# Retention and top-2 experts on one Trainium2 core: gathered rows transposed ahead of the next chunk's rows, weight sums ahead of routing steps, third-sequence routing behind the first expert products

## Chip, core and metric

The kernel runs on one core of one Trainium2 chip. The metric is the device time of one execution in microseconds (us), lower being better. Three runs of the kernel before gave 706.69, 709.57 and 719.4 us, a median of 709.57.

## What is computed

A retention layer (a linear attention with a decay for each head) over 4 sequences of 768 tokens feeds a mixture of 8 experts, of which every token takes the best 2. Cut to its core:

```python
for t in range(S):                       # retention, 4 sequences, 8 heads of 64
    state = gamma * state + k[:, :, t, :, None] * v[:, :, t, None, :]
    y[:, :, t] = scale * einsum('bhd,bhde->bhe', q[:, :, t], state)
x = y as rows of 512                      # 3072 tokens
noisy = x @ w_gate + log1p(exp(x @ w_noise)) * noise
top2, weights = best two of 8 and their softmax
for e in range(8):                        # 512 -> 1024 -> 512
    out[mask] += weight * (relu(x[mask] @ w1[e]) @ w2[e])
```

## The kernel before

**Two phases.** The first runs over 24 chunks of 128 tokens, 6 for each of the four sequences (b = 0 to 3). The second runs over the experts: gather the rows of an expert's tokens, transpose them, two products, scale, add into the output by an indirect DMA. Expert 0 is split into pieces by the order in which its tokens become known: slots 0 to 383 come from the first two sequences, slots to 575 from the third, the rest from the fourth. So its work can start before the routing of the last tokens is finished.

**A chunk.** In the loop of lines 682 to 706, pass j issues: the score products of chunk j+1 (`qk`, L311), the scaled values and queries on POOL (`v_scale`, `q_scale`, L285, L291), the loads of chunk j+4 on SP (L226), the finishing of chunk j-1 (`x_hi` on ACT L350, `x_lo` on VectorE L354, `x_out` on SP: a transposing DMA L359 and a store to `xbuf` L360), the masked scores of chunk j+1 (`masked`, VectorE L318), whatever the table `between` holds for j, the products of chunk j (`y_mm`, L325 to L336, then copies of the state and a sum of squares on ACT, L342 and L345), the router logits of chunk j-3 (L366, L369), and whatever the table `todo` holds for j. Every engine runs its own instructions in exactly that order; nothing is reordered later. A row that waits holds up all rows behind it on its engine.

**Routing of a sequence** is a chain of small steps: `route_a` (logits out of PSUM, L379 to L388), `route_b` and `route_b2` (the best two, L396 to L418), `places` (running counts on TensorE, L425, L428), `route_c`, `route_h` (gates, L435 to L454), `route_d` (slots, L461 to L483), `route_e` and `products` (one-hot tables, L494, L496, L503), `table` (12 matmuls, L513), `route_f` (adds the table into `acc`, L520), `slots` (token numbers and weights, L526 to L536). After `slots` an indirect DMA on POOL gathers rows of `xbuf` (`gather`, L626), and a transposing DMA on SP writes them as columns into `xe` (`x_t`, L633).

**Weights of expert 0** are brought in during the chunk phase. `w_load` (SP, L176) fetches a quarter, `w_sum` (ACT, L180) sums its squares, `w_scale` adds the four sums over the partitions by a matmul (L184) into a corner of the PSUM tile `pR` and makes a power-of-two scale of them on VectorE, `w_hi` (ACT, L197) and `w_lo` (VectorE, L202) split the weights into two float16 parts. For the second matrix the low parts are made by `w_lo_pool`: a scaling on ACT (L209) and a subtraction on POOL (L210). The tile `pR` also holds the tables (L513) and the running counts.

**Between the phases** (lines 787 to 845) a list `units` holds the products of expert 0's early pieces: eight `mm1` of 384 columns (L729 to L731, then ACT L732 and VectorE L733), three `mm2` (L759 to L761, then ACT L745), eight `mm1` of 192 columns, one more `mm2`. `early(n)` issues the next n of them. The routing steps of the third and fourth sequence are written between the calls. Before, nine units are issued ahead of `table` of the third sequence, and two more ahead of `table` of the fourth. After the fourth table come the gathers of the last piece, the expert order (`ranks`), its loads into registers on SP (L848) and the loads of expert 1's weights (L850, L851, issued by L176). PSUM tiles for `mm1` rotate through three buffers (`pA`, shared with the scores), so the fourth `mm1` waits until VectorE has finished with the first.

Of the kernel before, what the change touches and what calls it, by code (L numbers as in the profile page):

```python
# [19 lines left out]
B, H, S, D = 4, 8, 768, 64  # L20
C = 128
NC = S // C
NCH = B * NC
# [11 lines left out]
B0 = B // 2  # L35
# [59 lines left out]
def moe_kernel(ctx, tc, qT, kT, kt, vt, noise, wgn, w1, w2, ctab, qtab, xbuf, out):  # L95
    nc = tc.nc
# [29 lines left out]
    onef = consts.tile([128, 128], F32, name="onef")  # L126
# [22 lines left out]
    SUM = pR[:, 480:488]  # L149
# [15 lines left out]
    ST, order = {}, []  # L165
# [13 lines left out]
        st, ss, sc = ST[which, e]  # L179
        nc.scalar.activation(junk, st[:, i * 1024:(i + 1) * 1024], AF.Square, accum_out=ss[:, i:i + 1])  # L180

    def w_scale(e, which):
        st, ss, sc = ST[which, e]
        nc.tensor.matmul(SUM[:, :4], onef, ss, start=True, stop=True, skip_group_check=True)  # L184
        s1 = work.tile([128, 1], F32, name="s1")
        nc.vector.tensor_reduce(s1, SUM[:, :4], axis=AX.X, op=OP.add)
        pow2(s1, TW1 if which == "1" else TW2, sc[:, 0:1], sc[:, 1:2])
# [17 lines left out]
    def w_lo_pool(e, which, i):  # L205
        st, ss, sc = ST[which, e]
        hi, lo = w_parts(which, i)
        s = st[:, i * 1024:(i + 1) * 1024]
        nc.scalar.activation(s, s, AF.Copy, scale=sc[:, 0:1])  # L209
        nc.gpsimd.tensor_tensor(lo, s, hi, op=OP.subtract)  # L210
# [151 lines left out]
    def logits(j):  # L362
        b, c = divmod(j, NC)
        v = int(b >= B0)
        for i in range(KT):
            nc.tensor.matmul(PL[:, c].rearrange("p s e -> p (s e)"), XT[j][:, i, :],  # L366
                             wg2[:, v, i].rearrange("p s e -> p (s e)"), start=(i == 0), stop=False,
                             skip_group_check=True)
            nc.tensor.matmul(PL[:, c, 0, :], XT[j][:, KT + i, :], wg2[:, v, i, 0, :], start=False, stop=(i == KT - 1),  # L369
                             skip_group_check=True)  # L370
# [85 lines left out]
    def route_d(b):  # L456
        oh, g, gr, cb, vv = R[b]
        s3 = [128, NC, NL]
        ov = work.tile(s3, F32, name="ov")
        sl = work.tile(s3, F32, name="sl")  # L460
        nc.vector.tensor_tensor(ov, POS[:, :NC, :], cb[:, 0:1, :].to_broadcast(s3), op=OP.is_ge)  # L461
        nc.vector.tensor_tensor(sl, POS[:, :NC, :], cb[:, 1:2, :].to_broadcast(s3), op=OP.add)
        ps = work.tile(s3, F32, name="ps")
        nc.vector.tensor_tensor(ps, POS[:, :NC, :], R["cum"][:, None, :].to_broadcast(s3), op=OP.add)
        nc.vector.scalar_tensor_tensor(ov, ov, BIG, sl, op0=OP.mult, op1=OP.add)
        cn = work.tile([128, NL], F32, name="cum")
        nc.vector.tensor_tensor(cn, POS[:, NC, :], R["cum"], op=OP.add)
        if b == B0 - 1:
            nc.vector.tensor_scalar(cn[:, E:E + 1], cn[:, 0:1], float(FIRST), None, op0=OP.max)
        if b == B - 2:  # L470
            nc.vector.tensor_scalar(cn[:, E + 1:NL], cn[:, E:E + 1], float(SECOND), None, op0=OP.max)
        R["cum"] = cn
        t = work.tile([128, 2, NC, NL], F32, name="t")
        nc.vector.tensor_tensor(t, oh, ov[:, None].to_broadcast([128, 2, NC, NL]), op=OP.mult)
        sf = work.tile([128, 2, NC], F32, name="sf")
        nc.vector.tensor_reduce(sf, t, axis=AX.X, op=OP.add)
        si = work.tile([128, 2, NC], I32, name="si")
        nc.vector.tensor_copy(si, sf)
        lb = work.tile([128, 2, 2, NC], I32, name="lb")
        nc.vector.tensor_scalar(lb[:, 0], si, 127, None, op0=OP.bitwise_and)  # L480
        nc.vector.tensor_scalar(lb[:, 1], si, 7, None, op0=OP.arith_shift_right)
        lf = work.tile([128, 2, 2, NC], BF, name="lf")
        nc.vector.tensor_copy(lf, lb)  # L483
        R[b] = (oh, g, ps, lf, vv)

    def route_e(b, k):

        if k == 0:
            R[b] += (work.tile([128, 2, NC, 128], BF, name="a", bufs=1),
                     work.tile([128, 2, NC, NV, NCOL], BF, name="bb", bufs=1),  # L490
                     work.tile([128, 2, NC, NCOL], BF, name="ob", bufs=1))
        oh, g, ps, lf, vv, a, bb, ob = R[b]
        s3 = [128, NC, NCOL]
        nc.vector.tensor_tensor(ob[:, k], blks[:, None, :].to_broadcast(s3), lf[:, 1, k, :, None].to_broadcast(s3),  # L494
                                op=OP.is_equal)
        nc.vector.tensor_tensor(a[:, k], lanes[:, None, :].to_broadcast([128, NC, 128]),  # L496
                                lf[:, 0, k, :, None].to_broadcast([128, NC, 128]), op=OP.is_equal)
        products(b, k, nc.vector, 0, 3)
# [68 lines left out]
    def route_g(b):  # L567

        oh, g, ps, lf, vv, a, bb, ob = R[b]
        sl = slice(b * NC, (b + 1) * NC)  # L570
        t = work.tile([128, 2, NC, NL], F32, name="t")
        nc.vector.tensor_tensor(t, oh, g[:, :, :, None].to_broadcast([128, 2, NC, NL]), op=OP.mult)
        nc.vector.tensor_tensor(gateb[:, sl], t[:, 0], t[:, 1], op=OP.add)
        t2 = work.tile([128, NC, NL], F32, name="t2")
        nc.vector.tensor_tensor(t2, oh[:, 0], oh[:, 1], op=OP.add)
        nc.vector.tensor_scalar(t2, t2, -BIG, BIG, op0=OP.mult, op1=OP.add)
        nc.vector.tensor_tensor(posb[:, sl], t2, ps, op=OP.add)
# [29 lines left out]
    todo = {}  # L607

    def at(j, f, *a):
        todo.setdefault(j, []).append((f, a))  # L610
# [25 lines left out]
    between = {}  # L636
    for b in range(B - 1):
        n = (b + 1) * NC
        steps = [(2, route_a, b), (3, route_b, b), (4, route_b2, b), (4, route_c, b), (4, route_h, b), (5, route_d, b),
                 (6, route_e, b, 0), (7, route_e2, b, 0), (7, route_e, b, 1), (8, route_e2, b, 1), (9, route_f, b),  # L640
                 (8, route_g, b)]
        if b == B - 2:
            steps = [(2, route_a, b), (3, route_b, b), (3, route_b2, b), (4, route_c, b), (4, route_h, b), (5, route_d, b)]
        else:
            between.setdefault(n + 9, []).append((table, b))
        between.setdefault(n + 5, []).append((places, b))
        if b == B0 - 1:

            steps = steps[:-2]
            between[n + 9] += [(route_f, b), (slots, 0, 3)]  # L650
            between[n + 9] += [(gather, 0, t, 0, 128, B0 * S) for t in range(2)]
            between.setdefault(n + 10, []).append((gather, 0, 2, 0, 128, B0 * S))
        for s in steps:
            at(n + s[0], *s[1:])
    at(0, gate_sum)
    at(1, gate_weights)
    for i in range(4):
        at((4, 7, 10, 12)[i], w_load, 0, "1", i)
        at((6, 9, 12, 14)[i], w_sum, 0, "1", i)
        at((15, 16, 17, 18)[i], w_hi, 0, "1", i)  # L660
        at((18, 19, 20, 22)[i], w_lo, 0, "1", i)
        at((14, 16, 17, 18)[i], w_load, 0, "2", i)
        at((16, 18, 19, 20)[i], w_sum, 0, "2", i)
        at(21 + i // 2, w_hi, 0, "2", i)
    at(2, nc.vector.tensor_copy, lanes, K("lanes"))
    at(2, nc.vector.tensor_copy, blks, K("blks"))
    between.setdefault(15, []).append((w_scale, 0, "1"))
    between.setdefault(21, []).append((w_scale, 0, "2"))
    at(22, w_lo_pool, 0, "2", 0)
    between[NCH - 1].append((w_lo_pool, 0, "2", 1))  # L670
    for t in range(2):
        at(NCH - 2, x_t, 0, t)
    between[NCH - 1].append((x_t, 0, 2))
    mid = SECOND // 128
    at(1, nc.sync.dma_start, xbuf[:128, :], zero.bitcast(F16))

# [31 lines left out]
    x_hi(NCH - 1)  # L708
    x_lo(NCH - 1)
    x_out(NCH - 1)  # L710
    route_g(B0 - 1)
    for i in range(7):
        zero_out(i)
    lctx.close()
# [20 lines left out]
    def out_scale(e, n0, n1):  # L735
        i2 = work.tile([128, 1], F32, name="i2")
        nc.vector.tensor_tensor(i2, ST["1", e][2][:, 1:2], ST["2", e][2][:, 1:2], op=OP.mult)
        if e not in GS:
            GS[e] = work.tile([128, NBLK], F32, name="gse")
        nc.vector.tensor_scalar(GS[e][:, n0:n1], wacc[:, NBLK * e + n0:NBLK * e + n1], i2, None, op0=OP.mult)  # L740
# [46 lines left out]
    b = B - 1  # L787
# [5 lines left out]
    def early(n):  # L793
        for _ in range(n):
            if units:
                units.pop(0)()

    w_lo_pool(0, "2", 2)
    w_lo_pool(0, "2", 3)
    early(1)  # L800
    logits(NCH - 3)
    route_e(b - 1, 0)
    products(b - 1, 0, nc.vector, 3, NV)
    early(1)
    logits(NCH - 2)
    early(2)
    logits(NCH - 1)
    route_a(b)
    early(1)
# [4 lines left out]
    products(b - 1, 1, nc.vector, 3, NV)  # L814
    early(2)
    places(b)
    out_scale(0, 0, 3)
    early(1)
    table(b - 1)
    route_c(b)  # L820
# [33 lines left out]
    for e in range(E):  # L854
        half = (CAPS[e] + 31) // 32 * 16
        cols = [(SECOND, CAPS[0])] if e == 0 else [(0, half), (half, CAPS[e])]
        n, more = 0, e + 1 < E
# [33 lines left out]
        todo = list(range(mid, NBLK)) if e == 0 else list(blocks(e))  # L891
# [30 lines left out]
    with tc.For_i(0, n_more) as i:  # L922
# [49 lines left out]
        for f in range(FT):  # L972
            ph = psum.tile([128, 128], F32, name="ph", tag="pA", bufs=3)
            for k in range(KT):
                nc.tensor.matmul(ph, w1t[:, k, f * 128:(f + 1) * 128], xt[:, k, :],
                                 start=(k == 0), stop=(k == KT - 1))
# [44 lines left out]
```

## Time and profile before

| | before |
|---|---|
| runs, median (lowest to highest) | 709.57 us (706.69 to 719.4) |
| the profiled execution | 707.5 us |
| its span, first to last instruction | 705.2 us |
| TensorE (PE) busy | 664.9 us, 94% |
| VectorE (DVE) busy | 300.8 us, 43% |
| ScalarE (ACT) busy | 298.3 us, 42% |
| GpSimd (POOL) busy | 220.9 us, 31% |
| chain that ended last | PE 80%, DVE 9%, DMA 4%, ACT 2%, SP's queue 2% |

The span is 2.3 us shorter than the execution's own time. The first 145 us are the chunk phase, the rest the experts, with expert 0's early pieces in between. PEclk is the granted clock of TensorE, 1.00 being full. In rows of the timeline the two numbers in front are the start and the length in us, and the bracket at the end is the idle time of that engine ahead of the row with what ended it. A row with x16 stands for 16 instructions.

### The profile page before, as it was taken

How to read it: one execution, taken by the hardware profiler on the slowest of the kernel's cores; microseconds unless marked ns; L12 is line 12 of the kernel's file. 1: busy time of each engine (PE TensorE's matmuls, PEld its weight loads, DVE VectorE, ACT ScalarE, POOL GpSimd, SP SyncE). 2: the span in 40 equal slices, each digit the busy share in tenths (PEclk: the TensorE clock that was granted, in tenths of full speed). 3: DMA queues.
4: the chain of work that ended last, by engine and by line, in shares of the span. 5: the costliest groups of instructions: out<-in, count | busy, mean ns of one | idle time of the engine just before them, and what ended most of it. 6: DMA issues, size and time to landing. Idle time of an engine off the chain costs nothing.

```text
span 705.2 us, 12301 instructions
## 1 busy us (share of the span) xinstructions
PE 664.9 (94%) x4949; PEld 411.2 (58%) x4949; DVE 300.8 (43%) x731; ACT 298.3 (42%) x540; POOL 220.9 (31%) x170
## 2 busy tenths in 40 slices
PE   8998798859999999999999999999999999999991
PEld 5998687735675554555455546554654565456540
DVE  4557969678743534352216221522252153215100
ACT  4553454452126743354344543544453554344110
POOL 4544635340352312420432044114302330330021
PEclk9999998779999999999999999999999999999997
DMA  9999999469289874676477266826672674472132
GB/s 329 318 319 323 358 345 298 122 152 355 46 222 257 149 239 74 111 178 165 79 132 217 95 120 115 275 35 115 107 270 47 127 203 135 75 132 32 16 46 31
DMA packets 116139, 119.25 MB, mean 169 GB/s; under 512 B 82609, under 2 KB 82865, under 8 KB 112497
## 3 DMA queue, kind: packets, MB, share of 16 engines
q1 hardware_dynamic: 104112, 91.25, 46.1%
q0 software_dynamic: 11392, 26.35, 20.2%
q8 instruction: 40, 0.66, 0.4%
q10 hardware_dynamic: 576, 0.85, 0.3%
q14 instruction: 19, 0.15, 0.1%
HBM read 72.80 MB, written 26.21 MB: 140 GB/s over the span
## 4 chain that ended last, share of the span: by engine, by line
PE 80%; DVE 9%; DMA 4%; ACT 2%; SPq 2%; issue 1%; POOL 0%; POOLq 0%; ACTq 0%
PE pH L729 12%; PE pH L730 12%; PE pH L731 12%; PE pO L759 11%; PE pO L760 11%; PE pO L761 11%; PE pY L325 3%; DMA wst<-w 2%; DVE am L318 2%; PE pA L311 2%; PE pY L329 2%; DVE x L354 1%; DVE bb L503 1%; PE pU L336 1%; DMA in_v<-vt 1%
## 5 line engine op out<-in xcount | busy, mean ns | idle before, releaser
L750 POOL DMA_INDIRECT out<-ot,idx x54 | 86.6, 1604 | 328.8 <-ACT ot L745 197.3
L729 PE MATMUL pH<-xe,w1h 128*128 128x384 f16 (+4 forms) x544 | 176.6, 325 | 9.0 <-DMA xe<-xg 7.8
L730 PE MATMUL pH<-xe,w1h 128*128 128x384 f16 (+4 forms) x544 | 176.7, 325 | 0.0
L731 PE MATMUL pH<-xe,w1l 128*128 128x384 f16 (+4 forms) x544 | 176.6, 325 | 0.0
L733 DVE SCALAR_TENSOR_TENSOR hl<-pH,hh 128x384 f16<-128x384 f32 (+4 forms) x136 | 74.3, 549 | 205.4 <-ACT hh L732 205.3
L761 PE MATMUL pO<-w2h,hl 128*128 128x512 f16 x384 | 145.5, 379 | 0.0
L760 PE MATMUL pO<-w2l,hh 128*128 128x512 f16 x384 | 145.5, 379 | 0.0
L759 PE MATMUL pO<-w2h,hh 128*128 128x512 f16 x384 | 145.5, 379 | 0.0
L732 ACT ACTIVATE hh<-pH 128x384 f16<-128x384 f32 (+4 forms) x136 | 65.7, 484 | 129.8 <-PE pH L731 127.6
L745 ACT ACTIVATE ot<-pO,gse 128x512 f32<-128x512 f32 (+4 forms) x54 | 37.1, 686 | 171.9 <-PE pO L761 167.4
L202 DVE SCALAR_TENSOR_TENSOR w1l<-wst,wsc,w1h 128x1024 f16<-128x1024 f32 x32 | 41.6, 1306 | 99.0 <-ACT w1h L197 99.0
L626 POOL DMA_INDIRECT xg<-xbuf,idx x55 | 57.9, 1052 | 66.6 <-DVE wacc L529 23.9
L729 PEld LDWEIGHTS <-w1h 128*128 128x128 f16 x544 | 54.0, 99 | 40.9 <-issue 8.7
L731 PEld LDWEIGHTS <-w1l 128*128 128x128 f16 x544 | 53.5, 98 | 34.6 <-issue 0.9
L730 PEld LDWEIGHTS <-w1h 128*128 128x128 f16 x544 | 53.4, 98 | 34.5 <-issue 2.1
L180 ACT ACTIVATE junk<-wst 128x1024 bf16<-128x1024 f32 x64 | 67.1, 1048 | 7.1 <-DMA wst<-w 6.9
L761 PEld LDWEIGHTS <-hl 128*128 128x128 f16 x384 | 37.5, 98 | 45.3
L759 PEld LDWEIGHTS <-hh 128*128 128x128 f16 x384 | 38.1, 99 | 44.0
L760 PEld LDWEIGHTS <-hh 128*128 128x128 f16 x384 | 37.5, 98 | 44.0
L325 PE MATMUL pY<-vp,am 128*128 128x64 f32 x384 | 50.2, 286 | 0.5
L325 PEld LDWEIGHTS pY<-vp,am 128*128 128x128 f32 x384 | 46.9, 199 | 3.2 <-DVE x L354 1.4
L285 POOL TENSOR_TENSOR vp<-in_v,ct 128x512 f32<-128x512 f32 x24 | 25.9, 1080 | 54.2 <-PE pU L336 27.2
(162 smaller groups left out, 702.1 us busy)
## 6 DMA issues: line engine op xcount, KB each, us to landing
wst<-w SPq DMA_DIRECT2D x28, 1024.0 KB, 7.5
in_q<-qT SPq DMA_DIRECT2D x24, 256.0 KB, 5.6
in_k<-kT SPq DMA_DIRECT2D x24, 256.0 KB, 6.1
in_v<-vt SPq DMA_DIRECT2D x24, 256.0 KB, 5.6
in_kt<-kt SPq DMA_DIRECT2D x24, 256.0 KB, 5.9
xbuf<-x SPq DMA_DIRECT2D x24, 256.0 KB, 4.9
out<-zero SPq DMA_DIRECT2D x6, 1024.0 KB, 8.4
wst<-w SPq DMA_DIRECT2D x8, 512.0 KB, 7.2
```

The source lines that it names most:

```text
L180: nc.scalar.activation(junk, st[:, i * 1024:(i + 1) * 1024], AF.Square, accum_out=ss[:, i:i + 1])
L325: nc.tensor.matmul(pY[:, 2 * i + s, :], AM[j][:, s, i, :], VP[j][:, 2 * i + s, :], start=(i == 0 and s == 0), stop=True, skip_group_check= ...
L626: nc.gpsimd.indirect_dma_start(out=x[:p1], out_offset=None, in_=xbuf[:128 + rows], in_offset=bass.IndirectOffsetOnAxis(ap=idx[:p1, i:i + 1 ...
L729: nc.tensor.matmul(p[:, :n], whi, xh, start=(k == 0), stop=False)
L730: nc.tensor.matmul(p[:, :n], whi, xl, start=False, stop=False)
L731: nc.tensor.matmul(p[:, :n], wlo, xh, start=False, stop=(k == KT - 1))
L732: nc.scalar.activation(hh[:, f, n0:n1], p[:, :n], AF.Relu)
L733: nc.vector.scalar_tensor_tensor(hl[:, f, n0:n1], p[:, :n], 0.0, hh[:, f, n0:n1], op0=OP.max, op1=OP.subtract)
L750: nc.gpsimd.indirect_dma_start(out=out, out_offset=bass.IndirectOffsetOnAxis(ap=idx[:n, i:i + 1], axis=0), in_=ot[:n], in_offset=None, com ...
L759: nc.tensor.matmul(p, a, WT["2h"][:, f, :], start=(f == 0), stop=False)
L760: nc.tensor.matmul(p, a, WT["2l"][:, f, :], start=False, stop=False)
L761: nc.tensor.matmul(p, c, WT["2h"][:, f, :], start=False, stop=(f == FT - 1))
```

## The change

No arithmetic changes; instructions change their places.

- `w_scale` is split: its matmul becomes `w_total`. For the second matrix it is issued before `route_f` instead of behind `slots` and two gathers; the rest of `w_scale` goes behind three gathers.
- The last `w_sum` of each matrix goes to the front of its pass's list (`todo[14]`, `todo[20]`), ahead of the routing step's functions on ACT.
- `w_hi` and `w_lo` of the first matrix move: quarters 0 and 1 of `w_lo` from passes 18 and 19 to 16 and 17.
- All three gathers of slots 0 to 383 are issued together in pass 21, and their three transposes at the end of pass 21 (before: two at the end of pass 22, one in pass 23).
- `route_d` of the third sequence, `route_g` of the second and all four `w_lo_pool` go behind the start of the first products, one between each two `mm1`; `out_scale(0, 0, 3)` goes forward with them.
- Ten units instead of nine are issued ahead of the third sequence's `table`; the last one ahead of the fourth sequence's `table` is now the first `mm1` of 192 columns.

```diff
-    def w_scale(e, which):
+    def w_total(e, which):
+        nc.tensor.matmul(SUM[:, :4], onef, ST[which, e][1], start=True, stop=True, skip_group_check=True)
+
+    def w_scale(e, which, total=True):
         st, ss, sc = ST[which, e]
-        nc.tensor.matmul(SUM[:, :4], onef, ss, start=True, stop=True, skip_group_check=True)
+        if total:
+            w_total(e, which)
...
         if b == B - 2:
-            steps = [(2, route_a, b), (3, route_b, b), (3, route_b2, b), (4, route_c, b), (4, route_h, b), (5, route_d, b)]
+            steps = [(2, route_a, b), (3, route_b, b), (3, route_b2, b), (4, route_c, b), (4, route_h, b)]
...
-            between[n + 9] += [(route_f, b), (slots, 0, 3)]
-            between[n + 9] += [(gather, 0, t, 0, 128, B0 * S) for t in range(2)]
-            between.setdefault(n + 10, []).append((gather, 0, 2, 0, 128, B0 * S))
+            between[n + 9] += [(w_total, 0, "2"), (route_f, b), (slots, 0, 3)]
+            between[n + 9] += [(gather, 0, t, 0, 128, B0 * S) for t in range(3)]
+            between[n + 9] += [(w_scale, 0, "2", False)]
...
-        at((15, 16, 17, 18)[i], w_hi, 0, "1", i)
-        at((18, 19, 20, 22)[i], w_lo, 0, "1", i)
+        at((15, 15, 16, 17)[i], w_hi, 0, "1", i)
+        at((16, 17, 20, 22)[i], w_lo, 0, "1", i)
...
-    between.setdefault(21, []).append((w_scale, 0, "2"))
-    at(22, w_lo_pool, 0, "2", 0)
-    between[NCH - 1].append((w_lo_pool, 0, "2", 1))
-    for t in range(2):
-        at(NCH - 2, x_t, 0, t)
-    between[NCH - 1].append((x_t, 0, 2))
+
+    for j, w in (14, "1"), (20, "2"):
+        todo[j].remove((w_sum, (0, w, 3)))
+        todo[j].insert(0, (w_sum, (0, w, 3)))
+    for t in range(3):
+        at(NCH - 3, x_t, 0, t)
...
-    route_g(B0 - 1)
...
-    w_lo_pool(0, "2", 2)
-    w_lo_pool(0, "2", 3)
+    w_lo_pool(0, "2", 0)
+    early(1)
+    w_lo_pool(0, "2", 1)
+    route_d(b - 1)
+    out_scale(0, 0, 3)
     early(1)
     logits(NCH - 3)
+    w_lo_pool(0, "2", 2)
+    route_g(B0 - 1)
+    early(1)
+    w_lo_pool(0, "2", 3)
     route_e(b - 1, 0)
     products(b - 1, 0, nc.vector, 3, NV)
     early(1)
     logits(NCH - 2)
-    early(2)
+    early(1)
     logits(NCH - 1)
...
     places(b)
-    out_scale(0, 0, 3)
     early(1)
     table(b - 1)
```

Three places show what moves on the engines. Functions of the changed kernel stand a few lines lower: its L637 is L633 before, L213 is L209, L735 is L732, L736 is L733, L524 is L520.

**SP, the end of the chunk phase.** `xt` is a chunk's own transpose (L359), `xe` that of gathered rows (L633); the four `xt` are those of chunks 20 to 23. Before:

```order
L359 DMA_TRANSPOSE xt<-x_1807 128x8x128
L360 DMA xbuf<-x_1807 128x1024
L359 DMA_TRANSPOSE xt<-x_1923 128x8x128
L360 DMA xbuf<-x_1923 128x1024
L633 DMA_TRANSPOSE xe<-xg 128x8x128 x2
L359 DMA_TRANSPOSE xt<-x_1992 128x8x128
L360 DMA xbuf<-x_1992 128x1024
L633 DMA_TRANSPOSE xe<-xg 128x8x128
L359 DMA_TRANSPOSE xt<-x_2055 128x8x128
```

Now:

```order
L363 DMA_TRANSPOSE xt<-x_1807 128x8x128
L364 DMA xbuf<-x_1807 128x1024
L637 DMA_TRANSPOSE xe<-xg 128x8x128 x3
L363 DMA_TRANSPOSE xt<-x_1928 128x8x128
L364 DMA xbuf<-x_1928 128x1024
L363 DMA_TRANSPOSE xt<-x_1991 128x8x128
L364 DMA xbuf<-x_1991 128x1024
L363 DMA_TRANSPOSE xt<-x_2030 128x8x128
```

The three gathered transposes now stand ahead of chunk 21's own, where two stood behind it and the third behind chunk 22's.

**ACT, from the last chunk's finish into the first products.** L350 finishes a chunk, L209 is the scaling of `w_lo_pool`, L732 the ReLU of an `mm1`. Before:

```order
L209 ACTIVATE wst_1281<-wst_1281,wsc_1283 128x1024
L350 ACTIVATE x_1992<-pY,upx 128x512
L209 ACTIVATE wst_1281<-wst_1281,wsc_1283 128x1024
L345 ACTIVATE junk,xss<-pY 128x512
L350 ACTIVATE x_2055<-pY,upx 128x512
L209 ACTIVATE wst_1281<-wst_1281,wsc_1283 128x1024 x2
L732 ACTIVATE hh<-pH 128x384 x4
```

Now:

```order
L354 ACTIVATE x_1991<-pY,upx 128x512
L349 ACTIVATE junk,xss<-pY 128x512
L354 ACTIVATE x_2030<-pY,upx 128x512
L213 ACTIVATE wst_1282<-wst_1282,wsc_1284 128x1024
L735 ACTIVATE hh<-pH 128x384
L213 ACTIVATE wst_1282<-wst_1282,wsc_1284 128x1024
L735 ACTIVATE hh<-pH 128x384
```

The chunks finish first, and each scaling stands ahead of one ReLU.

**VectorE, around the fourth sequence's table.** `bb` is the one-hot product for that table, `acc` the row that reads it, `hl` the second half of an `mm1`'s output. Before:

```order
L503 TENSOR_TENSOR bb<-ob,vv 128x6x168
L520 TENSOR_TENSOR acc<-acc,pR 128x280
L526 TENSOR_TENSOR tk<-acc 128x3
L535 TENSOR_SCALAR padv<-tk,ct 128x3
L536 SCALAR_TENSOR_TENSOR idx<-tk,padv 128x3
```

Now:

```order
L507 TENSOR_TENSOR bb<-ob,vv 128x6x168
L736 SCALAR_TENSOR_TENSOR hl<-pH,hh 128x192
L524 TENSOR_TENSOR acc<-acc,pR 128x280
L530 TENSOR_TENSOR tk<-acc 128x3
L539 TENSOR_SCALAR padv<-tk,ct 128x3
L540 SCALAR_TENSOR_TENSOR idx<-tk,padv 128x3
```

One `mm1` of 192 columns, which reads the gathered rows of the third sequence, now stands ahead of the fourth table, on TensorE as on VectorE.

## The prediction

> **What bounds the kernel now.** I read the stages first: the span cut where the work changes, with the busy time of each engine in the order PE, PEld, DVE, ACT, POOL, then the granted TensorE clock and the DMA share.
>
> ```profile
> 84.00:100.00 16.00, 13.26 (x152) 11.93 (x151) 9.96 (x50) 7.03 (x19) 5.18 (x6) 0.89 1.17 308
> 100.00:131.00 31.00, 23.90 (x248) 21.57 (x249) 30.31 (x66) 16.01 (x32) 15.32 (x11) 0.89 0.92 267
> 131.00:153.00 22.00, 14.64 (x151) 13.81 (x150) 13.11 (x66) 11.37 (x20) 8.34 (x6) 0.75 0.58 144
> 153.00:215.00 62.00, 60.37 (x431) 39.25 (x432) 41.93 (x129) 15.84 (x35) 19.71 (x15) 0.95 0.68 210
> 215.00:684.00 469.00, 469.00 (x3013) 253.59 (x3011) 151.84 (x276) 205.94 (x335) 126.20 (x93) 1.00 0.58 130
> ```
>
> From 215 us on TensorE never stops and its clock is full; nothing edited touches that, so the change is worth what it moves the 215 us mark. Ahead of it, VectorE is full from 100 to 131 us (30.31 of 31.00), and from 131 to 153 us no engine is. Then the waits of TensorE between 80 and 215 us: total, times, longest.
>
> ```profile
> PE pH L729 <- DMA xe<-xg: 7.8, 1, 7.8
> PE pA L311 <- DVE am L318: 4.5, 3, 3.0
> PE pR L184 <- DVE acc L520: 3.2, 1, 3.2
> PE pR L184 <- ACT junk L180: 2.7, 1, 2.7
> PE pH L729 <- DVE hl L733: 1.2, 1, 1.2
> ```
>
> The change is aimed at the first, third and fourth: 13.7 us. The waits also cost clock:
>
> ```profile
> 130.56 0.36 PE L184 MATMUL pR<-wss,onef 128*128 128x4 f32 x2 [3.21 <-DVE acc L520]
> 130.77 2.81 PE L325 MATMUL pY<-vp,am 128*128 128x64 f32 x16
> 138.65 2.00 PE L325 MATMUL pY<-vp,am 128*128 128x64 f32 x16
> ```
>
> The same sixteen products take 2.81 us behind the wait of 3.21, and 2.00 a chunk later; the stage's 0.75 over 22 us is 5.5 us of clock.
>
> **Part 1, the first matrix's sum (about 86 us).** The matmul L184 waits for a square sum that stands on ACT behind `route_a`'s exponentials, which wait for VectorE:
>
> ```profile
> 86.68 0.24 ACT L387 ACTIVATE sp<-lg 128x48 f32<-128x48 f32 x1 [2.39 <-DVE lg L384]
> 87.11 1.04 ACT L180 ACTIVATE junk<-wst 128x1024 bf16<-128x1024 f32 x1
> 100.00 0.79 DVE L435 TENSOR_SCALAR dn<-den 128x6 f32<-128x6 f32 x1 [2.44 <-ACT den L418]
> ```
>
> Put first, the sum starts at 86.68 - 2.39 = 84.3 and ends near 85.5, inside ACT's idle 2.39 us, when the table's matmuls end too. TensorE is 2.7 us earlier, and keeps its clock: the stage's 0.89 is 1.8 us over 16. The 2.7 and some 1.4 of that clock bring the end of chunk 16's products 4.1 forward. `den` on ACT stands right behind chunk 16's copies and sum, so it comes as much earlier; ACT also makes two quarters of `w1h` in pass 15 now, ahead of chunk 15's finish, but these end before chunk 16's products do. VectorE's L435, which waits for `den`, goes from 100.0 to 96.0: **minus 4.0** (0 if the loads or VectorE hold the chunks back, 4.5 with all the clock).
>
> **Part 2, the VectorE stage (100 to 131 us).** The work of VectorE there is unchanged: two `w1l` rows move from passes 18 and 19 to 16 and 17, inside the same full stage. TensorE's wait of 3.0 for `am` becomes two or three of 1 to 2 us. So the stage keeps its length and the 4.0 are carried through:
>
> ```profile
> 129.97 0.44 DVE L520 TENSOR_TENSOR acc<-acc,pR 128x280 f32<-128x280 f32 x1
> 130.91 0.16 DVE L536 SCALAR_TENSOR_TENSOR idx<-tk,padv 128x3 int32<-128x3 f32 x1
> ```
>
> `acc` falls to about 125.7 and the indices to 126.6 (I allow 0.3 more for shorter contention with POOL). TensorE no longer waits for `acc` ahead of chunk 21; its gain there (3.2, and some 3 of clock) is larger than VectorE's, but the last chunks then wait for VectorE's `am` and POOL's values, so chunk 23's products end about 134.5.
>
> **Part 3, the gathered rows (to the first product).**
>
> ```profile
> 131.36 1.15 POOL L626 DMA_INDIRECT xg<-xbuf,idx  x1 [4.71 <-DVE wacc L530]
> 132.81 0.98 POOL L626 DMA_INDIRECT xg<-xbuf,idx  x1 [0.30 <-issue]
> 137.79 0.97 POOL L626 DMA_INDIRECT xg<-xbuf,idx  x1
> xg<-xbuf,idx POOLq DMA_INDIRECT x9, 3.4
> 150.18 1.30 SPq L633 DMA_TRANSPOSE xe<-xg  x1
> 150.18 3.08 DMA xe<-xg
> 153.40 0.48 PE L729 MATMUL pH<-xe,w1h 128*128 128x384 f16 x1 [7.76 <-DMA xe<-xg]
> ```
>
> Now the third transpose waits until 150.18 for chunk 22's on SP. In the changed kernel the three gathers start at 126.9, 128.3 and 129.6, the third lands 3.4 to 4.5 later (133.0 to 134.1), and its transpose 3.1 after that, 136.1 to 137.2. First product at **136.6 against 153.40: minus 16.8**, after a wait of some 2 us. Two queues pay. On SP, chunk 21's transpose waits behind the third gather until 135; its logits are read behind two units, so nobody waits. On POOL the third gather's 1.3 us stand ahead of chunk 23's values, which are ready as VectorE's mask is.
>
> **Part 4, first product to third table.** Now:
>
> ```profile
> 177.78 1.43 PE pR L513 x12
> 179.21 0.22 PE pO L759
> 189.57 1.44 PE pR L513 x12
> 206.04 6.64 DMA wst<-w
> 214.63 0.27 PE pH L729
> ```
>
> First product to the table's end is 179.21 - 153.40 = 25.8. One `mm2` more stands ahead of this table; two of them take 189.57 - 179.21 = 10.36, so plus 5.2. The clock's 0.95 over 62 us is 3.1; with a wait of 2 instead of 7.8 us I keep 1.0 of it: minus 2.1. And VectorE gets work between the products that was behind the chunks:
>
> ```profile
> 146.93 4.20 POOL L210 TENSOR_TENSOR w2l<-wst,w2h 128x1024 f16<-128x1024 f32 x2 [8.16 <-ACT wst L209]
> 149.31 1.96 DVE L474 TENSOR_TENSOR t<-oh,ov 128x120 f32<-128x120 f32 x1
> 179.25 0.22 DVE L461 TENSOR_TENSOR ov<-pR,cb 128x60 f32<-128x60 f32 x1 [1.63 <-PE pR L513]
> 179.88 0.28 DVE L474 TENSOR_TENSOR t<-oh,ov 128x120 f32<-128x120 f32 x1
> 181.00 0.18 DVE L483 CAST lf<-lb 128x24 bf16<-128x24 int32 x1
> 159.25 0.50 DVE L494 TENSOR_TENSOR ob<-blks,lf 128x336 bf16<-128x336 bf16 x1
> 160.54 1.97 DVE L503 TENSOR_TENSOR bb<-ob,vv 128x1008 bf16<-128x1008 bf16 x2
> ```
>
> The same row takes 0.28 us alone and 1.96 beside L210, ending when L210 ends. Four L210 of 2.1 us now follow one another from about 140 to 148, beside `route_d` and `route_g`; I let three rows be held, 1.7 each, and with 1.9 of `route_d` (179.25 to 181.2), 1 of the five small rows of `route_g` (an estimate from these) and 3.2 of `route_e` (159.25 to 162.5) the third `mm1`'s `hl` comes at 149 and the fourth's at 153. The sixth and seventh `mm1` wait for those buffers, 1.3 and 2.2 us: plus 3.5 (0 if VectorE is never held, 6 if each L210 holds a row). [...] Sum: 25.8 + 5.2 - 2.1 + 3.5 = 32.4, so the table ends at 169.0, **minus 10.2**.
>
> **Part 5, third table to 215 us.** Behind the third table VectorE makes the next indices, POOL gathers two blocks, SP transposes them. The new order puts the first 192-column `mm1`, which needs them, ahead of the fourth table.
>
> ```profile
> 183.73 1.13 POOL L626 DMA_INDIRECT xg<-xbuf,idx  x1 [0.30 <-issue]
> 192.03 0.33 ACT L732 ACTIVATE hh<-pH 128x192 f16<-128x192 f32 x1 [1.73 <-PE pH L731]
> 193.02 0.33 ACT L732 ACTIVATE hh<-pH 128x192 f16<-128x192 f32 x1 [0.66 <-PE pH L731]
> ```
>
> From the table's end: 1.1 to the indices (as from `acc` to `idx` above; `route_d` of the fourth sequence is done by then), 1.5 to the second gather, 3.4 and 3.1 of DMA, 9.1 in all; one `mm2` of 5.2 covers part, so TensorE waits 3.9. Then one `mm1` (193.02 - 192.03 = 1.0) and the table, 1.4: 11.5 from table to table at full clock, 12.6 if the wait of 3.9 leaves them at half speed for most of their length; I take 12.2. Before, it is 189.57 + 1.44 - 179.21 = 11.8. Lost: **0.4**. From the fourth table on the chain is unchanged: expert order, registers, the weights of expert 1 (206.04), their square sum, the product at 214.63; TensorE has 1.0 less to do in it, which that chain does not pass on. [...]
>
> **The sum.** 16.8 gained to the first product; 5.2 + 3.5 - 2.1 = 6.6 given back to the third table, 0.4 to the fourth: 9.8. The profiled execution's 707.5 (span 705.2 and 2.3 around it) becomes 697.7. The median of the runs shown is 709.57, 2.1 above it; I put half of that on and round: **699 us**.
>
> **Rivals.**
> A: VectorE keeps up. Its holds fall between waits, and the 3.5 and the remaining 1.0 of clock vanish: gain 14.3, 693.2. For it: VectorE is busy only 41.93 of 62 in that stage. Against: the rows it would run are of the kind held at 149.31.
> B: the gain of part 1 is lost on the way. DMA share is 1.17 from 84 to 100 us, so the loads may not come 4 us sooner, or POOL holds VectorE more often; `acc` stays at 130. Then the third gather starts at 134.0 and lands by 138, the first product is at 141 (gain 12.4), and after the 7.0 given back 5.4 are left: 702. Against: no wait of TensorE on a load is among the rows above.
> C: slower. The units are dealt out for the worse: the extra `mm2` (5.2), VectorE held by every L210 (6.0) and the wait ahead of the fourth table at half clock (0.8) cost 12.0, less 2.1 of clock, 9.9. This decides as soon as the first product gains under 9.9, that is, when the third gathered block's columns land later than 143.5. With columns at 146 it is 2.5 over: 710. For it: three gathers, three transposes and chunk 21's row go through one SP queue in order, and a late gather holds them all. Against: 3.4 us for a gather, 9 us of room.
> D: the change doesn't do what it says, the first product still waits for a chunk's transpose. The order on SP excludes it.
>
> **Chances.** The sum 0.52 (own range 694.5 to 701.5), A 0.20, B 0.20, C 0.08. The range of 692 to 706 leaves out most of C and the tails. 2% of 709.57 is 14.2 us, about what a measurement of this kernel can tell from no change: under 695.4 lie most of A and a tenth of the sum, 0.22; over 723.8 a corner of C, 0.02; within, 0.76.
>
> **What would show it.** Right: no wait of TensorE on L180 at 86 us and none on `acc`; `acc` near 126; first product near 137 after about 2 us; waits of the sixth and seventh 384-column `mm1` on `hl`; a wait near 4 us on `xe` in front of the fourth table; the fourth table near 180; no wait after 215 us less ten. Wrong: `acc` still at 130; a first product later than 141; no wait on `hl` (then A); or a loss behind the fourth table, where I have none.

## The result and the profile after

| | before | after |
|---|---|---|
| runs, median (lowest to highest) | 712.31 us (706.69 to 726.07, 20 runs) | 708.09 us (703.37 to 714.41, 20 runs) |
| time, after to before | 1 | 0.9942, 95% interval 0.9924 to 0.9959 |
| the profiled execution | 707.5 us, span 705.2 | 708.31 us, span 706.1 |

The change gains about 0.6%, 4 us, where 10.6 were forecast (709.57 to 699). The two profiled executions can't show these 4 us: that of before lies 4.8 us under the median of its runs, that of after 0.2 over its own. What they show is at which places the gain came and went.

The stages after, in the columns of the prediction's first fence (span part, then PE, PEld, DVE, ACT, POOL, the granted clock, DMA share, GB/s):

```profile
84.00:100.00 16.00, 15.49 (x185) 13.95 (x184) 14.12 (x62) 10.51 (x22) 6.46 (x7) 1.00 1.15 308
100.00:131.00 31.00, 29.80 (x284) 27.59 (x285) 29.22 (x77) 14.53 (x32) 15.38 (x12) 0.72 0.98 286
131.00:153.00 22.00, 15.72 (x150) 11.74 (x150) 17.69 (x54) 14.10 (x22) 11.02 (x7) 0.99 0.93 260
153.00:215.00 62.00, 53.28 (x366) 34.89 (x365) 35.01 (x119) 11.53 (x29) 15.53 (x13) 0.92 0.54 161
```

From 84 to 100 us the clock is whole, as forecast. From 153 to 215 us TensorE, which had been busy for 60.37 us, is busy for 53.28: there are new waits. TensorE's waits between 80 and 220 us:

```profile
PE pH L732 <- DVE hl L736: 6.3, 3, 4.2
PE pH L732 <- DMA xe<-xg: 5.8, 2, 5.5
PE pA L315 <- DVE am L322: 2.3, 2, 1.4
PE pY L329 <- DVE dn L439: 1.7, 1, 1.7
PE pO L764 <- DVE hl L736: 0.6, 1, 0.6
PE pH L732 <- issue: 0.5, 1, 0.5
PE pR L183 <- ACT junk L180: 0.3, 1, 0.3
```

The 3.2 for `acc` are gone, and of the 7.8 for the gathered rows and the 2.7 for the square sum 0.3 each are left. In their place stand 6.3 for VectorE's low halves `hl`, 1.7 ahead of the last chunk's products (`dn`), and 5.5 for gathered rows at another place. The timeline shows that place, between the third table (at 172.88) and the fourth (at 187.02):

```profile
172.88 1.59 PE L517 MATMUL pR<-bb,a 128*128 128x280 bf16 x12
185.14 0.32 PE L732 MATMUL pH<-xe,w1h 128*128 128x192 f16 x1 [5.49 <-DMA xe<-xg]
187.02 3.00 PE L517 MATMUL pR<-bb,a 128*128 128x280 bf16 x12
```

The first 192-column product waits for the rows of the third table, and the fourth table stands behind it in TensorE's order. The table then runs at half speed (3.00 instead of 1.59 us).

The chain of waits, in order of time (start, length, what), is this from the gathers on, with VectorE as its longest part between first product and third table:

```profile
131.88 4.16 DMA xg<-xbuf,idx
136.05 3.26 DMA xe<-xg
139.36 0.34 PE pH L732
144.86 1.89 DVE t L478
147.09 1.68 DVE si L482
148.79 2.04 DVE lb L484
173.04 1.44 PE pR L517 x12
177.72 3.27 DMA xg<-xbuf,idx
182.37 2.73 DMA xe<-xg
187.22 2.80 PE pR L517 x12
205.28 7.04 DMA wst<-w
```

The account of the two profiles, in us (a table's end is read from the first VectorE row behind it):

| | before | after | moved |
|---|---|---|---|
| first product | 153.40 | 139.36 | -14.0 |
| third table's end | 179.25 | 174.51 | -4.7 |
| fourth table's end | 191.04 | 190.06 | -1.0 |
| first product behind the next weights' sum | 214.63 | 214.27 | -0.4 |

14.04 us are gained, and 9.30, 3.76 and 0.62 given back.

### The profile page after: what moved, and what is told of

Its sections match the earlier page's. It is cut to its first block, busy times and chain, and to the rows that moved or that the text cites. A ratio compares the mean times of both kernels' runs of the same rounds, so it can differ in the third digit from the quotient of the medians.

```text
span 706.1 us, 12302 instructions
## 1 busy us (share of the span) xinstructions
PE 667.3 (95%) x4949; PEld 412.6 (58%) x4949; DVE 301.3 (43%) x731; ACT 298.0 (42%) x540; POOL 220.1 (31%) x170
## 4 chain that ended last, share of the span: by engine, by line
PE 78%; DMA 8%; DVE 5%; issue 2%; SPq 2%; POOL 1%; ACT 1%; POOLq 0%; ACTq 0%
PE pH L734 11%; PE pH L732 11%; PE pH L733 11%; PE pO L764 11%; PE pO L762 11%; PE pO L763 11%; PE pY L329 4%; DMA wst<-w 3%; PE pA L315 2%; DMA in_q<-qT 2%; PE pY L333 1%; DMA xg<-xbuf,idx 1%; PE pU L340 1%; DMA xe<-xg 1%; DMA in_v<-vt 1%
## 5 line engine op out<-in xcount | busy, mean ns | idle before, releaser
L732 PE MATMUL pH<-xe,w1h 128*128 128x384 f16 (+4 forms) x544 | 176.8, 325 | 12.7 <-DVE hl L736 6.3
L733 PE MATMUL pH<-xe,w1h 128*128 128x384 f16 (+4 forms) x544 | 176.6, 325 | 0.0
L736 DVE SCALAR_TENSOR_TENSOR hl<-pH,hh 128x384 f16<-128x384 f32 (+4 forms) x136 | 74.3, 549 | 209.1 <-ACT hh L735 207.5
L735 ACT ACTIVATE hh<-pH 128x384 f16<-128x384 f32 (+4 forms) x136 | 65.2, 483 | 134.5 <-PE pH L734 132.9
L630 POOL DMA_INDIRECT xg<-xbuf,idx x55 | 57.6, 1047 | 73.2 <-DVE wacc L533 31.4
L733 PEld LDWEIGHTS <-w1h 128*128 128x128 f16 x544 | 53.5, 98 | 41.1 <-issue 8.5
L732 PEld LDWEIGHTS <-w1h 128*128 128x128 f16 x544 | 54.1, 99 | 38.5 <-DMA xe<-xg 5.6
```

Source lines behind the costliest of these rows:

```text
L630: nc.gpsimd.indirect_dma_start(out=x[:p1], out_offset=None, in_=xbuf[:128 + rows], in_offset=bass.IndirectOffsetOnAxis(ap=idx[:p1, i:i + 1 ...
L732: nc.tensor.matmul(p[:, :n], whi, xh, start=(k == 0), stop=False)
L733: nc.tensor.matmul(p[:, :n], whi, xl, start=False, stop=False)
L735: nc.scalar.activation(hh[:, f, n0:n1], p[:, :n], AF.Relu)
L736: nc.vector.scalar_tensor_tensor(hl[:, f, n0:n1], p[:, :n], 0.0, hh[:, f, n0:n1], op0=OP.max, op1=OP.subtract)
```

## The experiments

All times are ratios to the kernel before, run beside each kernel on the same chip. "First product" to "fourth table" are from one profile of each kernel, and single profiles differ: the change, e1 to e5, n1 and b1 have the same program up to the `acc` ahead of the first gathers, and it comes between 125.12 us (n1) and 127.77 us (the change). A difference of two us at one mark shows little by itself. The stretch from first product to third table is steadier: 35.2, 35.3 and 33.9 us in the change, e5 and f1, whose programs agree there.

| run | first product | third table's end (behind the product) | fourth table's end (behind the third) | time to before, 95% interval |
|---|---|---|---|---|
| before | 153.40 | 179.25 (25.9) | 191.04 (11.8) | 1 |
| after | 139.36 | 174.51 (35.2) | 190.06 (15.6) | 0.9942 (0.9924 to 0.9959) |
| e1, nine units | 138.77 | 168.73 (30.0) | 180.52 (11.8) | 0.9832 (0.9798 to 0.9867) |
| e2, places used sooner | 139.37 | 174.45 (35.1) | 187.56 (13.1) | 0.9901 (0.9868 to 0.9935) |
| e3, both | 138.43 | 170.37 (31.9) | 182.16 (11.8) | 0.9856 (0.9820 to 0.9892) |
| e4, low parts early | 139.70 | 171.79 (32.1) | 187.52 (15.7) | 0.9896 (0.9859 to 0.9934) |
| e5, ten units, rows later | 137.85 | 173.10 (35.3) | 185.35 (12.3) | 0.9929 (0.9902 to 0.9957) |
| n1, no subtraction | 138.78 | 168.00 (29.2) | 183.76 (15.8) | 0.9875 (0.9849 to 0.9900) |
| p1, sums alone | 146.37 | 172.23 (25.9) | 184.02 (11.8) | 0.9866 (0.9822 to 0.9911) |
| p2, gathers alone | 146.00 | 177.99 (32.0) | 189.78 (11.8) | 0.9968 (0.9938 to 0.9997) |
| p3, order alone | 149.31 | 185.24 (35.9) | 200.85 (15.6) | 1.0174 (1.0131 to 1.0216) |
| f1, fill at 100 us | 138.66 | 172.53 (33.9) | 188.10 (15.6) | 0.9980 (0.9953 to 1.0007) |
| b1, e1 with e4 | 137.79 | 166.08 (28.3) | 177.87 (11.8) | 0.9816 (0.9762 to 0.9869) |
| f2, b1 with f1 | 140.01 | 167.54 (27.5) | 179.33 (11.8) | 0.9800 (0.9772 to 0.9828) |

**e1: nine units ahead of the third table.** The theory: the new order between the phases gives the gain back. The rival: what lies behind the fourth table holds the end wherever the tables are.

```diff
     places(b)
-    early(1)
     table(b - 1)
```

> The changed kernel with nine units instead of ten ahead of the third table, as before the change; so the first 192-column product stands behind the fourth table again. Theory (the ten units are what gives the gain back): the third table ends about 5.2 us sooner after the first product (30 instead of 35.1), and between third and fourth table no product waits for the new gathers, so they lie 11.8 us apart again instead of 15.5; the 215 us mark moves to about 206 and the time to 0.983 of before (700 us). Rival (what lies behind the fourth table, the chain from the ranks to the next weights, holds the end wherever the tables are): the tables come sooner but the time stays at 0.994.

The theory held, nearly to the number: 30.0 us to the third table instead of 35.2, tables 11.8 us apart, 0.9832. The rival is out: of the 9.5 us that the fourth table gains, 9.2 reach the load of the next weights (196.05 instead of 205.28), and the median falls by 1.1%, 7.8 us. In e1's timeline the two tables, with only two second products between them and no wait:

```profile
167.11 1.59 PE L517 MATMUL pR<-bb,a 128*128 128x280 bf16 x12
178.89 1.59 PE L517 MATMUL pR<-bb,a 128*128 128x280 bf16 x12
```

**e2 and e3: the fourth sequence's places used sooner.** With the tenth unit (e2), and with nine (e3, whose places also come one unit sooner).

```diff
     places(b)
+    route_c(b)
+    route_h(b)
+    route_d(b)
     early(1)
     table(b - 1)
-    route_c(b)
-    route_h(b)
-    route_d(b)
```

> The changed kernel with the fourth sequence's routing steps C, H and D ahead of the tenth unit and the third table. Theory (route_d stands behind the table because both use one PSUM tile, and delays the row numbers behind the table): the third table's row numbers come 1.0 instead of 3.0 us after its end, the wait of the first 192-column product for the gathered rows falls from 5.5 to 3.5 us, the time by 2 us to 0.991. Rival (VectorE has no room there, so the third table then waits for route_d): the table ends later by what the row numbers gain, time unchanged at 0.994.

> The changed kernel with nine units ahead of the third table and the fourth sequence's places, routing steps C, H and D one unit sooner, ahead of the ninth. Theory: both gains, tables 11.8 us apart or a little less since route_d is no longer between them, third table 5 us sooner; 0.981 of before (698.5 us). Rival (route_d was hidden behind the two units between the tables once there are nine): the same as with nine units alone, 0.983; or, if the third table waits for route_d, slower than that by up to 3 us.

e2 gained what the theory had priced, by its median; its interval, 0.9868 to 0.9935, overlaps a little with that of the change. In the changed kernel `route_d` starts at the third table's end, behind a wait of 5.68 us for TensorE:

```profile
174.51 0.22 DVE L465 TENSOR_TENSOR ov<-pR,cb 128x60 f32<-128x60 f32 x1 [5.68 <-PE pR L517]
176.36 0.44 DVE L524 TENSOR_TENSOR acc<-acc,pR 128x280 f32<-128x280 f32 x1
177.29 0.16 DVE L540 SCALAR_TENSOR_TENSOR idx<-tk,padv 128x2 int32<-128x2 f32 x1
```

In e2 it is done before the table, and the first read behind the table is `acc` itself:

```profile
168.67 0.21 DVE L465 TENSOR_TENSOR ov<-pR,cb 128x60 f32<-128x60 f32 x1
174.45 0.45 DVE L524 TENSOR_TENSOR acc<-acc,pR 128x280 f32<-128x280 f32 x1 [3.85 <-PE pR L517]
175.39 0.17 DVE L540 SCALAR_TENSOR_TENSOR idx<-tk,padv 128x2 int32<-128x2 f32 x1
```

Counts and table share one PSUM tile, `pR`, in different columns, and in the changed kernel the step that reads the counts waited those 5.68 us for the table that stands ahead of it in the program. The wait for the rows fell from 5.5 to 3.7 us; the fourth table still ran at about half speed (2.98 us beside 1.59 in e1). e3 brought nothing beyond e1 (0.9856 beside 0.9832, intervals that overlap), as its rival had it: there the third table waits for `route_d` (1.6 us), and between the tables nothing waits for the rows any more.

**e4 and n1: GpSimd's subtractions.** e4 puts the four low parts back where they stood; n1 leaves the subtraction out.

```diff
# e4
+    at(22, w_lo_pool, 0, "2", 0)
+    between.setdefault(NCH - 1, []).append((w_lo_pool, 0, "2", 1))
...
-    w_lo_pool(0, "2", 0)
+    w_lo_pool(0, "2", 2)
+    w_lo_pool(0, "2", 3)
     early(1)
-    w_lo_pool(0, "2", 1)
...
-    w_lo_pool(0, "2", 2)
...
-    w_lo_pool(0, "2", 3)
# n1
-        nc.scalar.activation(s, s, AF.Copy, scale=sc[:, 0:1])
-        nc.gpsimd.tensor_tensor(lo, s, hi, op=OP.subtract)
+        nc.scalar.activation(lo, s, AF.Copy, scale=sc[:, 0:1])
```

> The changed kernel with GpSimd's four low parts of the second matrix where they were before the change: two during the last chunks, two ahead of the first product. Theory (GpSimd's adjoining subtractions hold VectorE's small steps from 142 to 151 us, and the products wait for VectorE): first product to third table falls from 35.1 to about 31 us, with hl waits of 2 us instead of 6.3; VectorE pays 1 to 2 us ahead of the first product, so the time falls by 2 to 3 us, to 0.990. Rival (the products wait because of their own number, not because VectorE is held): 35 us stays, and the time is the same or up to 2 us longer, 0.994 to 0.997.

> The changed kernel without GpSimd's four subtractions: the low part of the first expert's second matrix is the scaled matrix itself (this part of the computation is changed), with as many ScalarE steps as before. Theory (while GpSimd subtracts, VectorE's small steps of 0.2 to 0.3 us take 1 to 2 us, and the fourth product waits for the low halves behind them): these steps fall to 0.2 to 0.3 us each, the wait of 4.2 us for hl falls below 1.5 us, the third table comes 3 to 5 us sooner after the first product, time 0.988 to 0.990. Rival (TensorE would wait for ScalarE's high halves or the third sequence's steps in any case): the table 1 us sooner or less, 0.993.

The theory held in n1, and in e4 in part (waits for `hl` of 4.2 us in all, where it had 2; its interval in time overlaps a little with that of the change). After, GpSimd subtracts without a break for 8.43 us, and VectorE's small steps beside it are long:

```profile
142.38 8.43 POOL L214 TENSOR_TENSOR w2l<-wst,w2h 128x1024 f16<-128x1024 f32 x4 [8.46 <-ACT wst L213]
143.56 1.02 DVE L469 SCALAR_TENSOR_TENSOR ov<-ov,sl 128x60 f32<-128x60 f32 x1
144.77 1.97 DVE L478 TENSOR_TENSOR t<-oh,ov 128x120 f32<-128x120 f32 x1
147.09 1.67 DVE L482 CAST si<-sf 128x12 int32<-128x12 f32 x1
148.79 2.04 DVE L484 TENSOR_SCALAR lb<-si 128x12 int32<-128x12 int32 x1
```

Without the subtraction (n1, whose line numbers are one lower) the same four steps, in the same place:

```profile
142.92 0.21 DVE L468 SCALAR_TENSOR_TENSOR ov<-ov,sl 128x60 f32<-128x60 f32 x1
143.31 0.27 DVE L477 TENSOR_TENSOR t<-oh,ov 128x120 f32<-128x120 f32 x1
143.94 0.17 DVE L481 CAST si<-sf 128x12 int32<-128x12 f32 x1
144.14 0.17 DVE L483 TENSOR_SCALAR lb<-si 128x12 int32<-128x12 int32 x1
```

6.70 us became 0.82, the waits of the first products for `hl` went, and the third table came 29.2 instead of 35.2 us behind the first product. So the subtractions cost the products 6 us there. In e4 they don't run during the last chunks, as I had thought; ScalarE's scalings come first, and the subtractions start at 137.8 instead of 142.4. That leaves one long held step beside them and is worth 3.1 us to the table:

```profile
137.81 4.21 POOL L214 TENSOR_TENSOR w2l<-wst,w2h 128x1024 f16<-128x1024 f32 x2 [5.62 <-ACT wst L213]
144.87 2.06 DVE L469 SCALAR_TENSOR_TENSOR ov<-ov,sl 128x60 f32<-128x60 f32 x1
```

**e5: ten units, but the rows needed later.** One unit instead of two ahead of the fourth table.

```diff
         route_e2(b, k)
-    early(2)
+    early(1)
     table(b)
```

> The changed kernel with ten units ahead of the third table, but only one unit (the third block's second product) between third and fourth table, so that the first 192-column product stands behind the fourth table as before the change. Theory (the loss between the tables is this product's wait for the gathered rows, on TensorE's queue ahead of the table): first product to third table stays at 35 us, the tables come 9 to 11 us apart instead of 13 to 15.5, and the time falls by 2 to 4 us to 0.990. Rival (with ten units VectorE's factors of the fourth table are late in any case): tables 13 us or more apart, time 0.993 to 0.996.

The tables moved together, to 12.3 us, more than the theory's 9 to 11, and the time is that of the rival, whose 13 us didn't come either: 0.9929, an interval that overlaps with that of the change. TensorE no longer waits for the rows; the fourth table now waits for its factors, from GpSimd and VectorE:

```profile
171.47 1.59 PE L517 MATMUL pR<-bb,a 128*128 128x280 bf16 x12
180.26 0.88 PE L517 MATMUL pR<-bb,a 128*128 128x280 bf16 x6 [2.01 <-POOL bb L507]
183.73 1.58 PE L517 MATMUL pR<-bb,a 128*128 128x280 bf16 x6 [2.60 <-DVE bb L507]
```

e1 and e5 issue the same units ahead of the fourth table; they differ in the side of the third table on which the tenth stands, and in time by 1%. So the wait for the rows is one form of a wider fault. Behind the third table VectorE and GpSimd need 10.6 us for the fourth table's factors (173.10 to 183.73). Two units of 5.2 cover nearly all of that. A unit ahead of the third table delays the start of this chain, and is missing from its cover.

**p1, p2, p3: each part of the change alone,** on the kernel before. p1 has the edits of the weights (the sums' places, `w_total`, the rest of `w_scale` behind the gathers, passes 15 to 17); p2 the gathers and transposes; p3 all that is written behind the chunk loop up to the third table, with the four low parts. Their diffs are the change's own hunks.

> The kernel before with only the weight sums and the first matrix's high and low parts moved. Theory (the order of the transposed pieces on the queue, not VectorE, sets the first product in the kernel before): the row numbers come 2 to 4 us sooner, the first product follows by no more than that because the third piece still stands behind the last chunk's transfers; first product 150 to 152, time 0.995 to 1.0. Rival (the row numbers set the first product): first product and time 4 us sooner, 0.994 or less.

> The kernel before with only the three gathers in a row and their transposes ahead of chunk 22's own. Theory: first product at 141 to 143 instead of 153.4, and, with nine units and the low parts where they were, nearly all of it kept: third table 9 to 11 us sooner, time 0.985 to 0.988. Rival (the gain can't be kept because VectorE's routing work or the weights' low parts end just behind the old first product): time 0.993 or more.

> The kernel before with only the order behind the chunks changed: the third sequence's step D and step G, the four low parts and the tenth unit behind the first products. Theory (this part is what gives the gain back): first product where it was or 1 us sooner, third table 7 to 9 us later after it than before, the first 192-column product waits for rows ahead of the fourth table; time 1.008 to 1.016, slower than before. Rival (the work moved away from VectorE ahead of the first product pays for it): time 0.998 to 1.003.

Two of my three theories fell. p1 gains 7.0 us at the first product while the row numbers gain 3.0 (127.95 beside 130.91), so its rival has the time right and not the mechanism; it keeps all of it and is faster than the whole change. POOL's rows, the first of before, the other three of p1:

```profile
136.60 1.04 POOL L285 TENSOR_TENSOR vp<-in_v,ct 128x512 f32<-128x512 f32 x1 [2.82 <-issue]
129.85 0.98 POOL L630 DMA_INDIRECT xg<-xbuf,idx  x1 [0.30 <-issue]
130.85 1.05 POOL L289 TENSOR_TENSOR vp<-in_v,ct 128x512 f32<-128x512 f32 x1
132.06 0.97 POOL L630 DMA_INDIRECT xg<-xbuf,idx  x1 [0.16 <-issue]
```

Before, chunk 23's values (L285 there) started at 136.60, and the third gather, behind them on POOL, at 137.79. Here they start at 130.85 and 132.06: the third gather comes 5.7 us sooner, without having been moved. Why the values come sooner was not tested; p1's TensorE no longer waits for `acc` (3.2 us before).

p2 has its first product at 146.00, 7.4 sooner, and no wait for rows, though its row numbers came 2.1 us later than before (133.02) with the same program up to them. But it gives 6.1 us of the gain back by the third table, as its rival said: VectorE ends the last chunk's `x_lo` only at 153.8, and then GpSimd's second pair of subtractions (154.12, 4.20 us) stands beside two of its steps, of 2.16 and 2.02 us:

```profile
PE pH L727 <- DVE hl L731: 8.2, 2, 6.0
```

p3 is 1.7% slower, a little beyond the theory's range: 35.9 us from first product to third table, 15.6 between the tables, the two sizes of the changed kernel. The three parts add up to -1.3 - 0.3 + 1.7 = +0.1%; the change has -0.6%, which is just within their intervals. **The first part gains, the third loses; the second gains little** (0.3%, interval 0.9938 to 0.9997).

**f1: the clock at 100 us.** Twelve extra products into unused columns, ahead of the score products in passes 18 and 19.

```diff
     for j in range(NCH):
+        for _ in range(12 if j in (18, 19) else 0):
+            nc.tensor.matmul(pL[:, 256:], warm[:, :128], warm[:, :256], start=True, stop=True, skip_group_check=True)
```

> The changed kernel with twelve extra 256-column products, into unused columns, ahead of chunk 19's and chunk 20's first matrix product, where TensorE waited 1.4 us for VectorE. Theory (the wait at 100 us is what halves the clock, and the slow products then hold VectorE back): granted clock 1.00 from 100 to 120 us, the third table's sum (acc) at 125.5 to 126.5 us instead of 127.8, time 1 to 2 us less, 0.991 to 0.993. Rival 1 (VectorE is the bound there, its 4.95 of 5 us are full at either clock): clock 1.00, time 0.994. Rival 2 (the clock falls without a wait, too): clock 0.5 in this stretch again, time 0.994 to 0.997.

The stage 100 to 131 us in f1's profile:

```profile
100.00:131.00 31.00, 28.07 (x319) 24.56 (x318) 30.26 (x87) 15.24 (x34) 18.69 (x14) 1.00 1.02 292
```

The clock stayed whole (0.72 after), and `acc` (of the second sequence's table; the expectation calls it the third) came at 125.73 instead of 127.77. The time did not fall: 0.998, above what the theory and both rivals had, with an interval that takes in 1. Of the 2.0 at `acc` 0.7 were left at the first product, since the transposing DMA ahead of it took 4.54 us instead of 3.26. The profiled execution is 1.0 us faster than that of the change; why the median isn't stays open. So the half clock there has a price at `acc`, and none that these runs show in the time.

**b1 and f2: what helped, together.**

> The changed kernel with nine units ahead of the third table and GpSimd's low parts where they were before the change (both of the edits that helped by themselves). Theory (they take away different waits): the first product at 139 to 140, the third table 27 us behind it instead of 30 and 32, tables 11.8 us apart; 3 us better than nine units alone, 0.979 (698 us). Rival (both shorten the same wait for VectorE's low halves hl): no better than nine units alone, 0.983.

> Nine units, the low parts early and the extra products together. By the first theory the clock is 1.00 from 100 to 120 us, acc at 125 to 126 us, and the time 0.979 to 0.981; by the rival that VectorE is the bound, 0.9816 as without the extra products.

b1 has the shorter way to the third table, if not quite the 27 us of the theory (28.3, tables 11.8 apart), and at 0.9816 is the best by its median without extra products; its interval, 0.9762 to 0.9869, doesn't set it apart from e1 alone. f2, 0.9800, can't be told from b1: its own clock fell to half from 114.6 to 121.4 us. Both beat both kernels, 697 to 699.5 us.

## Why the prediction was wrong, step by step

- **Part 1, right.** The wait on the first matrix's sum is 0.3 instead of 2.7 us, the stage's clock 1.00, and VectorE's `dn` came at 96.41; 96.0 was forecast.
- **Part 2, half.** `acc` came 2.2 us sooner, not 4.3. Of the two or three waits of TensorE for `am` that were forecast one came, 1.4 us, and I had given them no cost in clock. Behind it the clock fell to half and the products of a chunk took 3.67 us instead of 1.98:

```profile
96.29 1.98 PE L329 MATMUL pY<-vp,am 128*128 128x64 f32 x16
101.20 2.07 PE L315 MATMUL pA<-qs,in_k 64*128 64x128 f32 x14 [1.39 <-DVE am L322]
103.20 3.67 PE L329 MATMUL pY<-vp,am 128*128 128x64 f32 x16
127.77 0.43 DVE L524 TENSOR_TENSOR acc<-acc,pR 128x280 f32<-128x280 f32 x1
```

  Most of the 2 us at `acc` are this clock's, and how long it lasted differed from profile to profile. From `dn` to `acc` it took 31.4 us in this profile, and 31.3 in that of e1, each with 17.1 us of half clock; 30.2 and 30.1 in b1 and e5 with 13.7; 29.7 and 29.1 in e4 and n1 with 6.8 (e2, with 6.8 and more waits for `am`, 30.4); 29.8 in f1 with none. But for f1 these are the same instructions; before, it took 30.0.
- **Part 3, right in kind.** Three gathers in a row, the first at 129.14, the third landing 4.2 us after its start, the transpose 3.3: first product at 139.36 instead of 136.6, -14.0 instead of -16.8. Along that chain 2.1 of the 2.8 missing are `acc`'s. But the last chunk's products, forecast to end at 134.5, ended at 139.0, and TensorE waited 0.35 us for the rows, not 2: sooner rows alone would have brought no more than that. These products started late, behind a wait of their own:

```profile
135.90 1.97 PE L329 MATMUL pY<-vp,am 128*128 128x64 f32 x16 [1.69 <-DVE dn L439]
```

- **Part 4, mechanism right, size too small.** VectorE was held by GpSimd and TensorE waited for `hl`. Three held rows of 1.7 us were forecast; four came, 6.70 us in all, and TensorE's cost is 6 us (n1), not 3.5. The tenth unit costs the 5.2 forecast (e1). First product to third table took 35.2 us, 32.4 were forecast. In n1, whose trace has no GpSimd instruction between 131.3 and 171.2 us, the same four steps take 0.82 us.
- **Part 5, the step that failed.** "`route_d` of the fourth sequence is done by then." It isn't: it reads the counts from the tile into which the table is being written, and stands behind the table. The profile of before shows that wait, and I had quoted the row (`ov`, idle for 1.63 us until L513) for another purpose. So the row numbers come 2.8 us behind the table instead of 1.1, TensorE waits 5.5 us instead of 3.9, and the fourth table runs at half clock: 15.6 us from table to table, where 12.2 were forecast and 11.8 stood before. e2 confirms the place of `route_d`: with it ahead of the table the wait is 3.7 us and the tables are 13.1 apart. e1 and e5 show the larger omission: I priced the tenth unit by its own 5.2 us and 0.4 more. To the fourth table it costs 9.0 us (35.2 and 15.6 beside e1's 30.0 and 11.8), and its price in time is 1.1% (0.9942 to 0.9832), 7.8 us, since it delays the chain to the fourth table and leaves one `mm2` fewer to cover it.
- **Behind the fourth table** another 0.6 us went, where I had none: 0.4 are the load of the next weights, 7.04 us instead of 6.64, and 0.2 lie ahead of it. No experiment was made on it.
- **The rivals.** A fell: VectorE did not keep up. B came half true, at `acc`. C's mechanism is what happened: it had 12.0 us of cost by the tenth unit, the held VectorE and the wait ahead of the fourth table (0.8 there, where 3.76 were measured), and 13.7 were measured to the 215 us mark. It stayed faster than before only because the first product gained 14.0, beyond the 9.9 at which C said the sign turns.

In sum, against the 9.8 us forecast: 2.76 less to the first product, 2.70 more to the third table, 3.36 more to the fourth and 0.62 behind it leave 0.36 at the 215 us mark. Behind the mark the profile of after takes 491.8 us to its end and that of before 490.6, so that it is the slower one by 0.8 in the whole. The runs show 4 us of gain: the profile of before lies 4.8 under its median, and where its other runs are longer no trace shows.

## What to carry to other kernels

Work that is put ahead of the head of a chain costs twice: it delays the chain, and it is missing where it used to cover it; here the tenth unit, 5.2 us by itself, cost 9.0 to the fourth table. Ask for each moved unit which chain it stood beside. Here a step that read one part of a PSUM tile waited 5.68 us for the writer of another part that stood ahead of it in the program, so a reader that may go first should be written first. Test the parts of a change alone: here one gained, one hardly did and one lost, and the whole was slower than its first part.

## What was not expected of the hardware

The clock fell to half after a wait of only 1.39 us, and stayed there for 17 us (101.2 to 118.3) though the trace has TensorE busy all that time. In e2 the same wait, 1.40 us at 101.23, left it whole, and behind one of 1.50, which ended at 107.31, it was half from 108.9 to 115.7; in f1 four waits of up to 1.2 us left it whole. Read from windows of 0.2 us between 84 and 216 us, the stretches at half clock lasted 3.4, 6.8, 6.8 and 10.2 us in the profile of before and 17.1, 3.4 and 6.8 us in that of after, and within each of the two all changes of the clock lie whole multiples of 3.41 us apart. A wait's length alone didn't decide here; what does, no run shows.

Two of the long steps beside GpSimd's subtractions have twelve elements per partition and a single input: a type conversion took 1.67 us in the profile of after and 0.17 in n1, an integer mask 2.04 and 0.17.
